# A channel attention with two MoE layers on one core: weight conversion rearranged in a hand-planned program

## Chip, core and metric

The program runs on one core of a Trainium2 chip. The metric is the device time of one execution in microseconds (us).

## What is computed

q, k and v are 6016 tokens by 256 channels, single precision. The weights come in double precision.

```
qn = q / (norm(q over tokens) + 1e-6);  kn likewise
s  = kn.T @ qn / tau                    # 256 x 256
a  = exp(s - max); a /= sum + 1e-9      # softmax over the last axis
x  = v @ a
h  = x @ w_in                           # 256 -> 2048
g  = (a0 + a1 h + a2 h^2 + a3 h^3) / (1 + |b0||h| + |b1| h^2 + 1e-6)
y  = g @ w_out                          # 2048 -> 256
out = (sigmoid(y @ w_gate) * (y @ w_val)) @ w_out2   # 256 -> 1536 -> 256
```

## The kernel before, in words

**Plan.** The kernel calls pl.op(engine, cost, vt, fn, reads, writes) for each step. Plan.schedule then runs a list schedule over these costs: among the steps that are ready on an engine, the one with the lowest vt goes first; a step with port=True also waits, in the plan, for the one port that DVE and POOL are taken to share. What comes out is a fixed order for each engine, and each engine serves its own in that order. The vt come from tables: VT (steps of the later blocks), VT0 (block 0) and WT (weights). The order on the chip is fixed by this; the times in the plan are not times of the chip.

**First part: q and k.** The 47 tiles of 128 tokens come in 15 chunks (LOADS) by DMA from SP's queue, laid out as k's first half, q, k's second half (512 columns). Each chunk lands in a buffer that a weight will fill later (STREAM). PE multiplies k by q into s_ps (s_mm, L405). ACT squares each pair of tiles (L415), DVE or POOL adds the squares to one of two sums in SBUF (L424, UNIT says which), and PE sums over the partitions with a product by ones into nrm (sum_mm, L388). Then comes a chain: square root (ACT, L464), a Newton step and reciprocals (norms, DVE), a product that spreads the norms (L477), scores (L488), exp (L498), transposes (L505), and the copy of the transposed weights of attention to SBUF (L515). The softmax's denominator goes into v's scale.

**Weights.** There are 17 pieces of 1 MB: four of W_in, four of W_out (wo), three each of wg, wv and wo2. Each holds 1024 double-precision words per partition. to_f32 turns a piece into single precision: ACT takes the high word's magnitude, scaled (Abs, L538); the low word's top bits are taken on ACT or by a shift on DVE (TOP, L541 or L545); the sign goes in on ACT, by a write into a 16-bit half of the low word (L550), or on DVE by a second step (SIGN, L556); DVE joins the parts by shift and or (L552). The result stands in a temporary in SBUF (IN_TMP, TMP). For the pieces of W_out and the second layer, split_weight makes a hi part rounded by ACT (L622) and a lo part, the difference, on DVE or POOL (LOW, L626). A W_in piece is first multiplied by the attention matrix (w_mm, L592), and its product is split from PSUM (L598 on ACT, L600 on DVE).

**Blocks.** Block 0 has 384 tokens, the eleven others 512. moe1 makes, for each of eight units j of 256 hidden columns, h in PSUM (L681 to L685), then on ACT u, abs and square (L691, L693, L695), a reciprocal's seed (L706) and an arctan (L711), on DVE six steps (v L697, w L700, Q L703, t L709, y L713, g L716), then hi (ACT, L719), lo (POOL, or DVE in block 0, L724) and the products with W_out (L732 to L742). evac_y takes y out (yhi L753, ylo L755). moe2 runs the second layer of a block while moe1 is at the next.

The DMA order of q/k chunks (x), weights (i, o, g, v, 2), constants (c) and the first v (n) is the string ORDER.

Of the kernel before, what the change touches and what calls it, by code (L numbers as in the profile page):

```python
# [225 lines left out]
def c_pool(n):  # L226
    return 0.147 + 0.002105 * n
# [7 lines left out]
def tile_channel_attention_two_moes(  # L235
# [15 lines left out]
    P = 128  # L251
# [114 lines left out]

    chunks = groups(T, LOADS[-1], LOADS[:-1])
# [4 lines left out]
    acc = {e: pl.buf("w", [P, 2, 2 * C], at=t_s) for e in "dp"}  # L372
# [23 lines left out]
    kqs = []
    for c, (t0, n) in enumerate(chunks):
        kq = pl.buf(STREAM[c], [P, n, 2 * C], at=-9000.0)
# [10 lines left out]
        pl.op(PE, 2 * n * c_pe(C, 4), t_s + c, s_mm, [kq], [s_ps])  # L409
    late = []  # L410
    for k, (c, i, n) in enumerate(units):
        kq, e = kqs[c], UNIT[k]
        fresh = k not in last and e not in of
        sq = acc[e] if fresh else pl.buf("a" if k % 2 else "s", [P, 2, 2 * C], at=t_s + k)
        pl.op(ACT, c_act(n * 2 * C, 0), t_s + c + .5, lambda kq=kq, i=i, n=n, sq=sq: nc.scalar.activation(  # L415
            out=sq.ap()[:, :n], in_=kq.ap()[:, i:i + n], func=ACTF.Square), [kq], [sq])
        if k in last:
            late.append((sq, n))
            continue
        of[e] = True  # L420
        if not fresh:
            eng = nc.vector if e == "d" else nc.gpsimd
            pl.op(DVE if e == "d" else POOL, c_dve(n * 2 * C) if e == "d" else c_pool(n * 2 * C), t_s + c + .6,
                  lambda sq=sq, n=n, x=acc[e], eng=eng: eng.tensor_tensor(  # L424
                      out=x.ap()[:, :n], in0=x.ap()[:, :n], in1=sq.ap()[:, :n], op=ALU.add),
                  [sq, acc[e]], [acc[e]], port=True)
    for e in sorted(of):
        pl.op(PE, 8 * .2, t_s + 99, sum_mm(acc[e], 2, False), [acc[e], "ones"], [nrm])
    for k, (sq, n) in enumerate(late):
        pl.op(PE, n * 4 * .2, t_n, sum_mm(sq, n, k == len(late) - 1), [sq, "ones"], [nrm])  # L430
# [16 lines left out]
    def newton(x, s, y, z, m):  # L447
# [28 lines left out]
    pl.op(DVE, 1.8, t_n, norms, [nrm, "sm_n", "cf", "ident", "sm_a"], [rn, "sm_k"], port=True)  # L476
# [52 lines left out]
    def to_f32(vt, wt, c, rkey, dst, key, n, how):  # L529
# [4 lines left out]
        def d(t=I32):  # L534
# [3 lines left out]
        pl.op(ACT, c_act(n, 0), vt, lambda: nc.scalar.activation(  # L538
            out=d(F32), in_=word(1, F32), func=ACTF.Abs, scale=DBL_EXP), [rkey], [key])
# [24 lines left out]
    ways = iter(zip(TOP, SIGN))  # L564
    win_v = words(w_in)
    for i, (c, n) in enumerate(WIN.cuts):
        load_w(WIN, win_v[:, :, c:c + n, :], i, "i")
        sb = pl.buf(IN_TMP[i], [P, 2 * CH], at=-4000.0 + i)
# [4 lines left out]
        to_f32(WT["ci"] + WT["ci_d"] * i, WIN, i, WIN.bufs[i][0], sbv, sb, 2 * n, next(ways))  # L573
# [30 lines left out]
    AT = {"o": -180.0, "g": -170.0, "v": -160.0, "2": -150.0}  # L604
    low, tmp = iter(LOW), iter(TMP)

    def split_weight(wt, src):
        x = {"wo": "o", "wg": "g", "wv": "v", "wo2": "2"}[wt.name]
        for i, (c, n) in enumerate(wt.cuts):
# [4 lines left out]
            sb = pl.buf(next(tmp), [P, 2 * CH], at=AT[x] + i)  # L614
# [248 lines left out]
```

## Time and profile before

| | us |
|---|---|
| median of 3 runs | 1256.24 (1251.53 to 1258.21) |
| the profiled execution, its own time | 1253.48 |
| its span in the profile | 1251.7 |
| first product with W_in starts (L592) | 69.10 |
| block 0's y is evacuated (L753) | 179.58 |

The profile shows one execution. Its span ends 1.8 us short of its time. Busy shares are means over the span, so they say little of a stage; windows and timelines do. A row of a timeline gives start, length, engine, line, operation, and in brackets how long the engine was idle before it and what it waited for.

### The profile page before, as it was taken

How to read it: one execution, taken by the hardware profiler on the slowest of the kernel's cores; microseconds unless marked ns; L12 is line 12 of the kernel's file. 1: busy time of each engine (PE TensorE's matmuls, PEld its weight loads, DVE VectorE, ACT ScalarE, POOL GpSimd, SP SyncE). 2: the span in 40 equal slices, each digit the busy share in tenths (PEclk: the TensorE clock that was granted, in tenths of full speed). 3: DMA queues.
4: the chain of work that ended last, by engine and by line, in shares of the span. 5: the costliest groups of instructions: out<-in, count | busy, mean ns of one | idle time of the engine just before them, and what ended most of it. 6: DMA issues, size and time to landing. Idle time of an engine off the chain costs nothing.

```text
span 1251.7 us, 13336 instructions
## 1 busy us (share of the span) xinstructions
PE 1180.9 (94%) x5170; PEld 974.4 (78%) x5170; DVE 997.4 (80%) x850; ACT 873.7 (70%) x1006; POOL 501.9 (40%) x254
## 2 busy tenths in 40 slices
PE   8762589999999999999999999999999999999998
PEld 7632578888878888888888888888888888888876
DVE  5877988848879979979979878978979979979811
ACT  6699877757757767767767757757757767767722
POOL 2301314434435435435435435435435435434422
PEclk9886699999999999999999999999999999999999
DMA  9950000000010010010010010010010000000000
GB/s 368 400 209 0 17 18 1 1 30 1 1 34 1 1 34 1 1 34 1 1 34 1 1 34 1 1 34 1 1 35 1 1 34 1 6 13 1 17 1 18
DMA packets 15601, 43.34 MB, mean 35 GB/s; under 512 B 1328, under 2 KB 1840, under 8 KB 14256
## 3 DMA queue, kind: packets, MB, share of 16 engines
q1 hardware_dynamic: 15536, 42.47, 9.0%
q8 instruction: 41, 0.67, 0.2%
q14 instruction: 24, 0.20, 0.1%
HBM read 36.31 MB, written 6.16 MB: 34 GB/s over the span
## 4 chain that ended last, share of the span: by engine, by line
PE 81%; DVE 9%; ACT 8%; DMA 1%; issue 1%; SPq 0%; DVEq 0%; ACTq 0%
PE pO L797 9%; PE pH L681 6%; PE pH L685 6%; PE pH L683 6%; PE pY L732 6%; PE pY L734 6%; PE pY L742 6%; PE pG L776 5%; PE pG L778 5%; PE pG L780 5%; PE pV L776 5%; PE pV L780 5%; PE pV L778 5%; PE pO L802 5%; DVE w L424 1%; DMA win<-in_moe_w_in_dram 1%
## 5 line engine op out<-in xcount | busy, mean ns | idle before, releaser
L790 POOL TENSOR_TENSOR lo<-sig,hi 128x512 fp32r<-128x512 f32 (+1 forms) x144 | 248.7, 1731 | 318.7 <-ACT hi L788 313.3
L724 POOL TENSOR_TENSOR lo<-w,hi 128x1024 fp32r<-128x1024 f32 (+1 forms) x90 | 219.9, 2443 | 309.3 <-ACT hi L719 240.4
L713 DVE SCALAR_TENSOR_TENSOR a<-a,s 128x1024 f32<-128x1024 f32 (+1 forms) x96 | 161.1, 1681 | 73.0 <-ACT a L711 73.0
L681 PE MATMUL pH<-vhi,win 128*128 128x512 f32 (+1 forms) x368 | 145.7, 396 | 28.5 <-DVE w L700 28.0
L732 PE MATMUL pY<-hi,wo 128*128 128x512 f32 (+1 forms) x384 | 152.3, 397 | 17.7 <-ACT hi L719 17.7
L711 ACT ACTIVATE a<-a 128x1024 f32<-128x1024 f32 (+1 forms) x96 | 99.8, 1042 | 94.2 <-DVE a L709 94.1
L709 DVE TENSOR_TENSOR a<-a,s 128x1024 f32<-128x1024 f32 (+1 forms) x96 | 162.8, 1699 | 1.8 <-ACT s L706 1.8
L693 ACT ACTIVATE a<-pH,cf 128x1024 f32<-128x1024 f32 (+1 forms) x92 | 101.8, 1107 | 83.8 <-PE pH L685 82.7
L797 PE MATMUL pO<-hi,wo 128*128 128x512 f32 (+1 forms) x576 | 151.4, 384 | 0.0
L734 PE MATMUL pY<-hi,wo 128*128 128x512 f32 (+1 forms) x384 | 151.3, 394 | 0.0
L683 PE MATMUL pH<-vlo,win 128*128 128x512 f32 (+1 forms) x368 | 144.6, 393 | 0.9 <-DVE vlo L657 0.9
L703 DVE SCALAR_TENSOR_TENSOR a<-a,s 128x1024 f32<-128x1024 f32 (+1 forms) x96 | 118.5, 1235 | 33.7 <-ACT s L695 33.4
L785 DVE TENSOR_TENSOR sig<-sig,pV 128x512 f32<-128x512 f32 (+1 forms) x144 | 96.4, 670 | 61.0 <-PE pV L780 61.0
L685 PE MATMUL pH<-vhi,win 128*128 128x512 f32 (+1 forms) x368 | 144.5, 393 | 0.0
L719 ACT ACTIVATE hi<-w 128x1024 fp32r<-128x1024 f32 (+1 forms) x96 | 100.6, 1048 | 51.8 <-PE pY L734 29.2
L716 DVE SCALAR_TENSOR_TENSOR w<-w,cf,a 128x1024 f32<-128x1024 f32 (+1 forms) x96 | 131.2, 1369 | 2.7
L797 PEld LDWEIGHTS pO<-hi,wo 128*128 128x128 f32 x576 | 107.6, 188 | 20.8
L700 DVE SCALAR_TENSOR_TENSOR w<-w,cf,pH 128x1024 f32<-128x1024 f32 (+1 forms) x92 | 116.3, 1264 | 1.2
L788 ACT ACTIVATE hi<-sig 128x512 fp32r<-128x512 f32 (+1 forms) x144 | 89.4, 628 | 37.0 <-DVE sig L785 20.4
L776 PE MATMUL pG<-yhi,wg 128*128 128x512 f32 (+1 forms) x288 | 112.2, 390 | 1.1 <-ACT yhi L753 1.1
L778 PE MATMUL pG<-ylo,wg 128*128 128x512 f32 (+1 forms) x288 | 111.4, 387 | 0.8 <-DVE ylo L755 0.8
L780 PE MATMUL pG<-yhi,wg 128*128 128x512 f32 (+1 forms) x288 | 111.4, 387 | 0.0
(176 smaller groups left out, 2334.0 us busy)
## 6 DMA issues: line engine op xcount, KB each, us to landing
wo<-in_moe_w_out_dram SPq DMA_DIRECT2D x7, 1024.0 KB, 14.4
v<-in_v_dram SPq DMA_DIRECT2D x11, 512.0 KB, 3.7
out_dram<-v SPq DMA_DIRECT2D x11, 512.0 KB, 2.8
wo<-in_kqk_dram SPq DMA_DIRECT2D x4, 1024.0 KB, 12.4
win<-in_moe_w_in_dram SPq DMA_DIRECT2D x4, 1024.0 KB, 16.7
wg<-in_kqk_dram SPq DMA_DIRECT2D x3, 1024.0 KB, 12.6
wv<-in_kqk_dram SPq DMA_DIRECT2D x3, 1024.0 KB, 17.4
wv<-in_moe_w_val_dram SPq DMA_DIRECT2D x3, 1024.0 KB, 13.8
```

The lines of the kernel that those rows point to most:

```text
L681: mm(out=hp.ap()[:, i, :n], lhsT=WIN.at(f * P, 0, z), rhs=vhi.ap()[:, z, :n], start=(z == 0), stop=False)
L683: mm(out=hp.ap()[:, i, :n], lhsT=WIN.at(f * P, 0, z), rhs=vlo.ap()[:, z, :n], start=False, stop=False)
L685: mm(out=hp.ap()[:, i, :n], lhsT=WIN.at(f * P, 1, z), rhs=vhi.ap()[:, z, :n], start=False, stop=(z == 1))
L709: pl.op(DVE, c_dve(N), vt + vp['t'] * d, lambda: nc.vector.tensor_tensor(out=V(a_), in0=V(a_), in1=V(s_), op=ALU.mult), [a_, s_], [a_], po ...
L724: lambda: e_lo.tensor_tensor(out=V(lo), in0=V(w_), in1=V(hi).bitcast(F32), op=ALU.subtract),
L732: mm(out=y_ps.ap()[:, z, :n], lhsT=WO.at(f * C, 0)[:, sl], rhs=hi.ap()[:, i, :n], start=(f == 0), stop=False)
L734: mm(out=y_ps.ap()[:, z, :n], lhsT=WO.at(f * C, 1)[:, sl], rhs=hi.ap()[:, i, :n], start=False, stop=False)
L776: mm(out=gp[i].ap()[:, :n], lhsT=wt.at(f * P, 0, z), rhs=yhi.ap()[:, z, :n], start=(z == 0), stop=False)
L778: mm(out=gp[i].ap()[:, :n], lhsT=wt.at(f * P, 0, z), rhs=ylo.ap()[:, z, :n], start=False, stop=False)
L780: mm(out=gp[i].ap()[:, :n], lhsT=wt.at(f * P, 1, z), rhs=yhi.ap()[:, z, :n], start=False, stop=(z == 1))
L790: pl.op(POOL, c_pool(n), vt + VT['lo2'] * d, lambda sg=sg, hi=hi, lo=lo: nc.gpsimd.tensor_tensor(out=lo.ap()[:, :n], in0=sg.ap()[:, :n], i ...
L797: mm(out=o_ps.ap()[:, z, :n], lhsT=WO2.at(f * C, i)[:, z * P:(z + 1) * P], rhs=hi.ap()[:, :n], start=(f == 0 and i == 0), stop=False)
```

## The change

It does five things.

1. The sign step of 7 of the 17 pieces (before 4) is a DVE step, put into the low word ahead of the join; ACT keeps 10.
2. The magnitudes of 11 pieces go into PSUM banks that are idle then (T_PS: H, Y, or 2 for the two halves in pG and pV); DVE joins from there. Squares that DVE adds up go through pH and pY too.
3. For 5 of the 15 chunks (KG is g; 13 of 47 tiles) only q is squared, and k's norms come from the diagonals of products of k with itself: s_mm multiplies 384 columns instead of 256 there, and diag_k picks the diagonals.
4. ORDER loads nine weight pieces among q and k; before, four W_in pieces stood there. The first v now comes last. The buffer of a chunk is picked by a rule instead of STREAM.
5. The hi part of 9 of 13 pieces is made by DVE (HI). The tables VT, VT0, WT are new, and block 1 and the second layer of block 0 have one of their own (VT1); the plan's cost of ACT's sign step is raised.

```diff
-ORDER = 'xxxxxxiccxxxxicxxixixxnoooovxgvgg222v'
+ORDER = 'xxvxxxvxxxxcxcgoixogxxxgixc22inovo2i'
+KG = 'ggsgssssssgsgss'
-IN_PS = 'Y2Y2'
+IN_PS = '2OYO'
-LO0 = 'dpdddddp'
+LO0 = 'ppppdpdp'
-TOP = 'adaadddaddadddddda'
-SIGN = 'ddddaaaaaaaaaaaaaa'
-LOW = 'pdddddppppddp'
+TOP = 'dadadadaaddaaddda'
+SIGN = 'daadaaadaadadaadd'
+HI = 'ddaaddddddada'
+LOW = 'pppppddpddddp'
+T_PS = 'H.2Y.Y.2HY.YH.Y.2'
...
-                    mm(out=s_ps.ap()[:, h, 0:C], lhsT=kq.ap()[:, i, h * (P + C):h * (P + C) + P],
-                       rhs=kq.ap()[:, i, P:P + C], start=(c == 0 and i == 0),
+                    lo_, hi_ = (h * P, h * P + P + C) if kg[c] else (P, P + C)
+                    mm(out=s_ps.ap()[:, h, lo_ - h * P:hi_ - h * P], lhsT=kq.ap()[:, i, h * (P + C):h * (P + C) + P],
+                       rhs=kq.ap()[:, i, lo_:hi_], start=(c == 0 and i == 0),
...
+        elif e == "d" and not direct:
+            sq = pl.buf("pH" if k % 2 else "pY", [P, 2, 512], at=t_s + c + i / 8)
...
+    def diag_k():
+        for h in range(2):
+            nc.vector.scalar_tensor_tensor(
+                out=rn.ap()[:, 2, :P], in0=s_ps.ap()[:, h, h * C:h * C + P], scalar=1.0, in1=ident, op0=ALU.mult,
+                op1=ALU.mult, accum_out=sm[:, 22 + h:23 + h])
...
+            pl.op(ACT, c_act(n // len(ts), 0), vt, lambda tv=tv, sl=sl: nc.scalar.activation(
+                out=tv(), in_=word(1, F32)[:, sl], func=ACTF.Abs, scale=DBL_EXP), [rkey], tt[1])
...
-            pl.op(ACT, c_act(n, 0), vt, lambda: nc.scalar.activation(
+            pl.op(ACT, .05 + .00215 * n, vt, lambda: nc.scalar.activation(
                 out=wt.half(c), in_=word(1, F32), func=ACTF.Copy, scale=SIGN_ONLY), [rkey, (rkey, 0)], [(rkey, 0)])
...
+                out=word(0), in0=word(1), scalar=-0x80000000, in1=word(0), op0=ALU.bitwise_and,
+                op1=ALU.bitwise_or), [rkey, (rkey, 0)], [(rkey, 0)], port=True)
+        for tv, tk, sl in ts:
+            pl.op(DVE, c_dve(n // len(ts)), vt, lambda tv=tv, sl=sl: V.scalar_tensor_tensor(
+                out=d()[:, sl], in0=tv(I32), scalar=3, in1=word(0)[:, sl], op0=ALU.logical_shift_left,
+                op1=ALU.bitwise_or), [rkey, (rkey, 0)] + tk, [key], port=t_ps == ".")
...
+            if next(high) == "a":
+                pl.op(ACT, c_act(a * m, 0), vt, lambda i=i, sv=sv: nc.scalar.activation(
+                    out=wt.part(i, 0), in_=sv(), func=ACTF.Copy), [sb], [key])
+            else:
+                pl.op(DVE, .07 + .00053 * a * m, vt, lambda i=i, sv=sv: nc.vector.tensor_copy(wt.part(i, 0), sv()),
+                      [sb], [key], port=True)
```

Three places show what the new tables do to the order. The first is SP's queue around the last chunks of q and k (rows with in_kqk_dram; a number is the buffer's). Before:

```order
L354 DMA wo_287<-in_kqk_dram 128x2048
L354 DMA win_311<-in_moe_w_in_dram 128x2x1024
L354 DMA wo_319<-in_kqk_dram 128x512
L354 DMA win_331<-in_moe_w_in_dram 128x2x1024
L354 DMA wg_339<-in_kqk_dram 128x512
L354 DMA wg_344<-in_kqk_dram 128x512
L354 DMA v<-in_v_dram 128x2x384
```

Now:

```order
L361 DMA win_335<-in_kqk_dram 128x2048
L361 DMA wo_340<-in_kqk_dram 128x512
L361 DMA wo_344<-in_kqk_dram 128x512
L361 DMA wg_346<-in_moe_w_gate_dram 128x2x1024
L361 DMA wg_366<-in_moe_w_gate_dram 128x2x1024
L361 DMA win_382<-in_moe_w_in_dram 128x2x1024
L361 DMA wv_399<-in_kqk_dram 128x512
```

Three more weight pieces stand between the last two chunks of q and k. The second place is ACT in block 0, where the first two units' seeds and arctans stand (L706 and L711; now L786 and L791). Before:

```order
L622 ACTIVATE wg_579<-yhi 128x1024
L550 ACTIVATE wo_513<-wo_513 128x1024
L550 ACTIVATE wo_547<-wo_547 128x1024
L706 ACTIVATE s<-a 128x2x384 x2
L550 ACTIVATE wo_564<-wo_564 128x1024
L538 ACTIVATE yhi<-wv_431 128x1024
L711 ACT_TABLE_LOAD
L711 ACTIVATE a<-a 128x2x384 x2
L550 ACTIVATE wv_462<-wv_462 128x1024
```

Now:

```order
L699 ACTIVATE wo_631<-hi 128x1024
L674 ACTIVATE win_636<-pO 128x512 x2
L612 ACTIVATE pV<-wo_524 128x512
L786 ACTIVATE s<-a 128x2x384
L674 ACTIVATE win_646<-pY 128x512 x2
L699 ACTIVATE wo_657<-lo 128x1024
L791 ACT_TABLE_LOAD
L791 ACTIVATE a<-a 128x2x384
L773 ACTIVATE a<-pO,cf 128x2x384
```

The last weight step on ACT is L699 of wo_657; behind it only steps of the blocks follow. The third place is DVE in the same stretch. Before:

```order
L545 TENSOR_SCALAR wv_577<-wv_577 128x1024
L552 SCALAR_TENSOR_TENSOR yhi<-yhi,wv_431 128x1024
L713 SCALAR_TENSOR_TENSOR a<-a,s 128x2x384 x2
L700 SCALAR_TENSOR_TENSOR w<-w,cf,pH 128x2x384
L700 SCALAR_TENSOR_TENSOR w<-w,cf,pO 128x2x384
L716 SCALAR_TENSOR_TENSOR w<-w,cf,a 128x2x384 x2
L552 SCALAR_TENSOR_TENSOR ylo<-ylo,wg_481 128x1024
```

Now:

```order
L676 TENSOR_TENSOR win_646<-pY,win_646 128x512 x2
L780 SCALAR_TENSOR_TENSOR w<-w,cf,pH 128x2x384
L793 SCALAR_TENSOR_TENSOR a<-a,s 128x2x384
L783 SCALAR_TENSOR_TENSOR a<-a,s 128x2x384
L796 SCALAR_TENSOR_TENSOR w<-w,cf,a 128x2x384
L777 TENSOR_TENSOR w<-w,pO 128x2x384
L789 TENSOR_TENSOR a<-a,s 128x2x384
```

Joins of weights (L552) stood between the units' steps; now the last weight step of DVE, L676 of win_646, is ahead of the first unit's w.

## Rows read from the trace of the kernel before

**Rows 1.** The page, part 1: busy time, share of the span and instructions of each engine.

```profile
PE 1180.9 (94%) x5170; PEld 974.4 (78%) x5170; DVE 997.4 (80%) x850; ACT 873.7 (70%) x1006; POOL 501.9 (40%) x254
```

**Rows 2.** Windows: stretch, its us, busy us (count) by engine, PEclk, DMA share, GB/s.

```profile
0.00:50.00 50.00, 43.42 (x198) 37.79 (x199) 35.99 (x31) 34.79 (x36) 19.58 (x14) 1.00 0.96 380
60.00:140.00 80.00, 39.99 (x135) 29.03 (x135) 61.14 (x69) 79.13 (x80) 13.61 (x5) 0.73 0.25 95
69.10:179.60 110.50, 65.70 (x237) 52.76 (x238) 92.34 (x96) 99.28 (x102) 17.74 (x7) 0.76 0.13 45
200.00:257.00 57.00, 56.60 (x282) 50.39 (x281) 44.24 (x41) 40.50 (x49) 27.13 (x16) 1.00 0.00 1
443.00:536.00 93.00, 93.00 (x410) 76.41 (x409) 79.36 (x64) 65.30 (x77) 40.84 (x20) 1.00 0.04 12
```

**Rows 3.** Timeline of PE, 0:180: start us, us, line, out<-in, count, [idle before <-releaser].

```profile
55.63 1.03 PE L388 MATMUL pV<-ones,s 128*128 128x1 f32 x8
...
69.10 5.92 PE L592 MATMUL pY<-hi,s 128*128 128x512 f32 x8 [2.13 <-ACT s L515]
...
109.01 0.66 PE L681 MATMUL pH<-vhi,win 128*128 128x384 f32 x1 [19.52 <-DVE w L700]
...
172.97 0.69 PE L732 MATMUL pY<-hi,wo 128*128 128x384 f32 x1 [2.86 <-ACT hi L719]
```

**Rows 4.** Timeline of ACT, 0:180.

```profile
47.65 0.63 ACT L415 ACTIVATE s<-wg 128x512 f32<-128x512 f32 x1 [1.85 <-DVE w L424]
...
56.70 0.17 ACT L464 ACTIVATE cf<-pV 128x4 f32<-128x4 f32 x1 [6.32 <-PE pV L388]
...
94.48 4.81 ACT L550 ACTIVATE wo<-wo 128x1024 f16<-128x1024 f32 x2
...
179.58 0.81 ACT L753 ACTIVATE yhi<-pY 128x768 fp32r<-128x768 f32 x1 [1.74 <-PE pY L742]
```

**Rows 5.** Groups by line and shape, 0:180: PE, ACT, DVE, POOL.

```profile
L405 PE MATMUL pO<-wo 128*128 128x256 f32 x84 | 20.6, 410 | 4.5 <-DMA wo<-in_kqk_dram 4.5
...
L550 ACT ACTIVATE wo<-wo 128x1024 f16<-128x1024 f32 x7 | 17.3, 2515 | 0.0
...
L538 ACT ACTIVATE v<-wo 128x1024 f32<-128x1024 f32 x5 | 5.7, 1178 | 0.9 <-DVE wo L626 0.9
L622 ACT ACTIVATE wo<-v 128x1024 fp32r<-128x1024 f32 x5 | 5.4, 1071 | 0.5 <-DVE v L552 0.3
...
L552 DVE SCALAR_TENSOR_TENSOR v<-v,wo 128x1024 int32<-128x1024 int32 x5 | 6.0, 1214 | 0.0
...
L545 DVE TENSOR_SCALAR wo<-wo 128x1024 int32<-128x1024 int32 x6 | 4.1, 688 | 0.0
...
L600 DVE TENSOR_TENSOR win<-pY,win 128x512 fp32r<-128x512 f32 x4 | 2.7, 686 | 1.9 <-ACT win L598 1.9
...
L626 POOL TENSOR_TENSOR wo<-v,wo 128x1024 fp32r<-128x1024 f32 x2 | 5.7, 2840 | 29.1 <-ACT wo L622 29.1
```

**Rows 6.** Timelines of DVE and of POOL, 0:180.

```profile
33.81 2.85 DVE L545 TENSOR_SCALAR win<-win 128x1024 int32<-128x1024 int32 x1
...
124.42 0.95 DVE L697 TENSOR_TENSOR w<-w,pH 128x768 f32<-128x768 f32 x1 [0.87 <-ACT w L691]
...
131.50 1.22 DVE L552 SCALAR_TENSOR_TENSOR ylo<-ylo,wv 128x1024 int32<-128x1024 int32 x1
...
134.50 1.22 DVE L552 SCALAR_TENSOR_TENSOR v<-v,wg 128x1024 int32<-128x1024 int32 x1
136.11 2.62 DVE L703 SCALAR_TENSOR_TENSOR a<-a,s 128x768 f32<-128x768 f32 x1 [0.40 <-ACT s L695]
...
32.89 3.22 POOL L424 TENSOR_TENSOR w<-w,a 128x1024 f32<-128x1024 f32 x1 [4.07 <-ACT a L415]
...
127.55 2.16 POOL L724 TENSOR_TENSOR lo<-w,hi 128x768 fp32r<-128x768 f32 x1 [1.60 <-ACT hi L719]
134.58 3.34 POOL L626 TENSOR_TENSOR wv<-ylo,wv 128x1024 fp32r<-128x1024 f32 x1 [4.87 <-ACT wv L622]
```

More of the change, by code (lines that the diff above doesn't have):

```diff
@@ L410, in tile_channel_attention_two_moes, with f @@
-    late = []
+        pl.op(PE, 2 * n * c_pe(P + C if kg[c] else C, 4), t_s + c, s_mm, [kq], [s_ps])
+    acc, late = {}, []
     for k, (c, i, n) in enumerate(units):
[L412 to L416, printed above, removed]
+        kq, e, g = kqs[c], UNIT[k % len(UNIT)], kg[c]
+        fresh = k not in last and (e, g) not in acc and n == (4 if g else 2)
+        direct = k in last or not fresh and (e, g) not in acc
+        if fresh:
+            sq = acc[e, g] = pl.buf("w" if e == "d" else "vhi" if g else "vlo", [P, 2, 2 * C], at=t_s + g)
+        elif e == "d" and not direct:
+            sq = pl.buf("pH" if k % 2 else "pY", [P, 2, 512], at=t_s + c + i / 8)
+        else:
+            sq = pl.buf("a" if k % 2 else "s", [P, 2, 2 * C], at=t_s + c + i / 8)
+        m = C if g else 2 * C
+        def f(t_, n=n, m=m):
+            return t_.ap().rearrange("p a c -> p (a c)")[:, :n * m].rearrange("p (a c) -> p a c", c=m)
+        pl.op(ACT, c_act(n * m, 0), t_s + c + .5, lambda kq=kq, i=i, n=n, sq=sq, f=f, g=g: nc.scalar.activation(
+            out=f(sq), in_=kq.ap()[:, i:i + n, P:P + C] if g else kq.ap()[:, i:i + n], func=ACTF.Square), [kq], [sq])
@@ L417, in tile_channel_attention_two_moes @@
         if k in last:
[L418 to L421, printed above, removed]
+            late.append((sq, n, g))
+        elif direct:
+            pl.op(PE, n * (2 if g else 4) * .2, t_s + c + .7, sum_mm(sq, n, g, False), [sq, "ones"], [nrm])
+        elif not fresh:
             eng = nc.vector if e == "d" else nc.gpsimd
[L423 to L430, printed above, removed]
+            pl.op(DVE if e == "d" else POOL, c_dve(n * m) if e == "d" else c_pool(n * m), t_s + c + .6,
+                  lambda sq=sq, x=acc[e, g], eng=eng, f=f: eng.tensor_tensor(out=f(x), in0=f(x), in1=f(sq), op=ALU.add),
+                  [sq, acc[e, g]], [acc[e, g]], port=e == "p")
@@ L432, in bcast @@
+    for (e, g), x in sorted(acc.items()):
+        pl.op(PE, 8 * .2, t_s + 99, sum_mm(x, 4 if g else 2, g, False), [x, "ones"], [nrm])
+    for k, (sq, n, g) in enumerate(late):
+        pl.op(PE, n * (2 if g else 4) * .2, t_n, sum_mm(sq, n, g, k == len(late) - 1), [sq, "ones"], [nrm])
     def bcast(src, n):
@@ L474, in norms @@
                                 scalar2=None, op0=ALU.mult)
-    pl.op(DVE, 1.8, t_n, norms, [nrm, "sm_n", "cf", "ident", "sm_a"], [rn, "sm_k"], port=True)
+    pl.op(DVE, 1.8, t_n, norms, ["sm_k2", "sm_n", "cf", "ident", "sm_a"], [rn, "sm_k"], port=True)
     pl.op(PE, c_pe(C, 4), t_n, lambda: mm(out=bc.ap()[:, 0:C], lhsT=ones, rhs=rn.ap()[:, 0, :],
@@ L602, in tile_channel_attention_two_moes @@
                 op=ALU.subtract), [ps[h], (key, 0, h)], [(key, 1, h)])
-    AT = {"o": -180.0, "g": -170.0, "v": -160.0, "2": -150.0}
-    low, tmp = iter(LOW), iter(TMP)
+    high, low, tmp = iter(HI), iter(LOW), iter(TMP)
     def split_weight(wt, src):
```

123 lines of the change are left out of this document (79 added, 44 removed).

## The prediction

> **What bounds the kernel now.** I read the page's busy shares first, then windows by stage, then the timelines of the stage that stands out, then the groups by line and shape for prices.
>
> PE is busy 94% of the span [rows 1], so little can be gained where it is already full. The windows say where it is not. From 200 us on PE is never free for long: 56.60 of 57, and in a whole block of 512 tokens 93.00 of 93 [rows 2]. In 60:140 it is busy 39.99 of 80, at a granted clock of 0.73, while ACT is busy 79.13 of those 80 [rows 2]. So the stage that can be shortened lies before 200 us: ACT sets its pace, and PE waits (19.52 us at 109.01, for a DVE step that in turn stood behind ACT) [rows 3]. What ACT does there is weight conversion standing among block 0's own steps, as with the pair of sign casts of 4.81 us at 94.48 [rows 4].
>
> Two marks cut the stage. **M1**, the first product of the attention matrix with W_in, is at 69.10 [rows 3]. **M2**, the evacuation of block 0's y, is at 179.58 [rows 4]. What PE has to do behind M2 is the same before and after: in the order 3841 rows of PE stand from the first matmul that reads yhi to the end, in both. So the time changes by as much as M2 moves, unless the later blocks' new order makes PE wait. I forecast M2, then weigh that condition as a rival.
>
> **M1, the stage that gets longer.** The last piece of q and k now comes behind nine weight pieces instead of four. A tile of q and k is 128x512 words of 4 bytes, 0.262 MB, and there are 47; a weight piece is 1.049 MB. Before: 12.3 + 4.2 = 16.5 MB, at the 380 GB/s of the first 50 us [rows 2] by 43.4 us; its square ran at 47.65, 4.2 later, of which 1.85 was idle time that DVE ended [rows 4]. After: 12.3 + 9.4 = 21.7 MB, by 57.3 us, so its square runs between 57.3 and 61.5; I take 59. With 0.63 for the square [rows 4] and two groups of sums at 1.03 [rows 3] the norms' sums end near 61.7, against 56.66 before (55.63 + 1.03). From there to M1 took 12.4 us, and the new chain differs by little: two sign casts and three Abs steps lie in it where three sign casts, an Abs step and a hi step did (2 x 2.52 + 3 x 1.18 = 8.6 against 3 x 2.52 + 1.18 + 1.07 = 9.8 [rows 5]), two small DVE steps on the diagonals come on top, and one more sign cast (2.52) stands ahead of the square root, which the sums may or may not outlast. **M1 = 74**, between 72 (no lag behind the transfer) and 79 (the full lag, and the sign cast ahead in full).
>
> Two costs lie beside this and are taken at nothing. The diagonals of k widen 26 products (13 tiles, two halves) from 256 to 384 columns: 26 x 0.205 = 5.3 us of PE, half of the 0.410 of a product [rows 5]. PE was busy 43.42 of the first 50 [rows 2]; it ends by about 53 with this, and the transfers cover it until 57; without that cover it would cost up to 5. The conversions that move ahead of M1 need ACT: 48 us of work in the 54 between the first and the last piece (18 whole squares at 1.05, nine Abs and five top-word steps at 1.18, four sign casts at 2.52, rest small). That fits, but not by much: the third rival.
>
> **M1 to M2, the stage that gets shorter.** It took 110.5 us, with ACT busy in 99.28 and DVE in 92.34 [rows 2]. In the new order no conversion stands among block 0's steps any more but for the first unit's, so I count what is left for each engine by the order.
>
> ACT: three sign casts (7.5), two whole and six half Abs (5.9), three top-word steps (3.4), four hi steps (4.3), eight W_in halves (5.0), four v casts (2.6), a table load (1.3), and eight units of block 0 of six steps, 43: 73 us. Of the 26 us that vanish, the sign casts are the largest part (ten of seventeen pieces against thirteen, and most of them now ahead of M1), then nine hi steps that went to DVE.
>
> DVE: twelve conversion steps of 1024 at 1.20 (14.4), fourteen half ones at 0.62 (8.7), four shifts and casts at 0.62 (2.5), four vlo steps (2.5), the first four steps of block 1 at 1.2 (4.8), and block 0. For that I take a run without gaps: from 124.42 to 134.50 stand ten steps of 768 columns and one conversion step, which takes 1.14 (131.50 to the next step) [rows 6], so a step takes (10.08 - 1.14)/10 = 0.894. Eight units of six and two lo steps: 50 x 0.894 = 44.7. Sum 77.6 us: **DVE is now the bound** of the stage, 4.6 ahead of ACT.
>
> On top come waits against POOL. While POOL runs, DVE steps with two operands in SBUF stretch: 2.62 instead of 0.96 at 136.11, beside the POOL step of 134.58 [rows 6]. Seven POOL steps lie in the old stage, and I count 5.6 us of stretch on DVE, 0.8 each; nine in the new one give 7. Steps that read PSUM were not stretched: the gapless run above holds a POOL step, 2.16 at 127.55 [rows 6]. More of them do now: I take 5, and 2 for other gaps. Ends: 0 and 0 (all of it falls beside PSUM steps), and 7 + 6 (a gap of 0.75 per unit). A cast of 1024 on DVE (two in this stage) is in no row: between the shift's 0.69 and a two-operand step's 1.21 [rows 5]; I take the shift, also one operand and all SBUF; the other end costs 1.
>
> The Trainium skill, "SBUF — State Buffer", section "Who interferes with whom", says that copy, cast and tensor_scalar steps in their two-port modes are shut out for the whole length of a GpSimd step. By it the nine casts moved to DVE are the change's weak spot; the sum by it is the second rival's.
>
> **M2 = 74 + 77.6 + 5 + 2 = 158.6**, which is 21.0 earlier. The profiled execution took 1253.48 (span 1251.7); minus 21.0 that is 1232.5. The median of the runs is 1256.24, 2.8 above the profiled one; on it the forecast is **1235 us**. With the low ends M2 = 149.6, 1226; with the high ends 79 + 78.6 + 13 = 170.6, 1247.
>
> **Rivals.**
> 1. *More.* The PSUM operands take away all stretch, ACT keeps up: M2 near 150, 1226. For it: the steps that read PSUM. Against it: t, y, Q and g of block 0 keep both operands in SBUF.
> 2. *DVE shut out.* Each one-operand step meets a POOL step, as the shift at 33.81 did: 2.85 instead of 0.69, beside POOL's 32.89 [rows 6]. Four such steps behind M1 lose 8.6, and the two-operand ones the full 7.2: 15.8 instead of 5, M2 169.4, 1246. Against it: nine POOL steps of some 2.84 [rows 5] fill under a third of the 85 us.
> 3. *No gain.* The conversions ahead of M1 don't fit: each queue is served in order, so an ACT step that waits for a late transfer holds the squares behind it, and POOL's sums, at 2.4 to 3.2 each, hold DVE. M1 at 90 gives M2 174.6, 1251, within what counts as no change.
> 4. *Slower.* The new tables reorder every block, not only the first. PE is full there, but DVE is busy 79.36 and POOL 40.84 of 93 [rows 2], and a unit's hi, lo and products hang in a chain; where PE meets a hi that isn't there it stands 2.86 us, as at 172.97 [rows 3]. Once more in each of eleven blocks: 31.5, and 1235 + 31.5 = 1267. It decides from 27 us on, 2.5 per block. Against it: DVE keeps 13.6 us of slack in a block, and the new order has the same steps per block, in much the same sequence.
>
> **How the numbers follow.** A measurement of this kernel can tell about 0.5% from no change, 6.3 us (1250.0 to 1262.5). Forecast 0.66 (1228 to 1243), rival one 0.10, two 0.10, three 0.07, four 0.07. The first three cases lie below 1250: faster 0.86; rival three is same, 0.07; rival four slower, 0.07. The range 1225 to 1249 takes in the forecast, rivals one and two and the ends of the unknown costs, and leaves out three and four and a little of the tails.
>
> **What would show it.** In the new profile: M1 between 72 and 79; no sign cast and no DMA-fed conversion behind the second unit of block 0; DVE busy for over 95% of M1 to M2 while ACT has gaps; M2 near 159; blocks from the third on still 93 us apart with PE full. An M2 over 170 with long one-operand DVE steps beside POOL would show rival two; an M1 over 85, rival three; PE idle inside later blocks, rival four. The forecast is wrong if M2 moves by 21 and the time doesn't.

## The result: 18 us faster, and the profile after

The changed kernel takes 1238.01 us (median of 4 runs, 1235.97 to 1242.28), the kernel before 1256.65 beside it: a ratio of 0.9863, with a 95% interval of 0.9824 to 0.9902. Run again beside later experiments it took 1236.69 (4 runs) against 1253.45, 0.9867 (0.9845 to 0.9889). The forecast was 1235, in a range of 1225 to 1249: faster, by about what was said. But M2 moved less than forecast, and the reason why is the more useful part.

The profiled execution of the changed kernel is the slowest of its first four (1242.28, span 1240.5), so the two profiles stand 11.2 apart and the medians 18.6. A second profile of the same kernel, taken with the runs below, has a span of 1235.7.

Page, part 1, and windows of the changed kernel (first profile), which answer to [rows 1, 2]:

```profile
PE 1192.8 (96%) x5202; PEld 978.7 (79%) x5202; DVE 999.0 (81%) x855; ACT 861.9 (69%) x998; POOL 523.0 (42%) x262
```

```profile
0.00:50.00 50.00, 45.67 (x182) 34.85 (x183) 25.67 (x18) 37.99 (x33) 26.48 (x17) 1.00 0.97 385
60.00:140.00 80.00, 54.86 (x193) 40.77 (x193) 70.03 (x105) 68.28 (x80) 16.58 (x8) 0.78 0.28 107
80.60:165.70 85.10, 62.58 (x237) 47.64 (x238) 78.06 (x88) 69.40 (x83) 19.68 (x9) 0.89 0.05 14
443.00:536.00 93.00, 93.00 (x410) 76.54 (x409) 78.86 (x63) 65.85 (x77) 41.12 (x20) 1.00 0.04 12
240.00:257.00 17.00, 13.71 (x47) 9.53 (x46) 12.11 (x11) 10.09 (x11) 2.40 (x1) 0.87 0.17 53
```

In 60:140 PE is busy for 54.86 us where it was for 39.99, and ACT is no longer full there (68.28 instead of 79.13). From M1 to M2 DVE is now the busiest engine, 78.06 of 85.10, where ACT was, 99.28 of 110.50. A later block is as full as before, 93.00 of 93.

Timeline of PE, changed kernel, answering to [rows 3]:

```profile
52.16 2.32 PE L426 MATMUL pO<-wo 128*128 128x384 f32 x8
55.60 1.95 PE L400 MATMUL pV<-ones,w 128*128 128x1 f32 x16 [1.11 <-DVE w L456]
57.41 3.12 PE L400 MATMUL pV<-ones,vlo 128*128 128x1 f32 x16
60.39 3.55 PE L400 MATMUL pV<-ones,vhi 128*128 128x1 f32 x16
63.80 2.05 PE L426 MATMUL pO<-wv 128*128 128x256 f32 x4
65.65 1.71 PE L400 MATMUL pV<-ones,a 128*128 128x1 f32 x8
67.21 1.84 PE L400 MATMUL pV<-ones,s 128*128 128x1 f32 x8
...
80.61 3.78 PE L668 MATMUL pG<-lo,s 128*128 128x512 f32 x4 [1.91 <-ACT s L560]
```

Timeline of ACT, changed kernel, answering to [rows 4]:

```profile
58.69 0.61 ACT L447 ACTIVATE s<-wv 128x512 f32<-128x512 f32 x1
...
69.35 0.20 ACT L509 ACTIVATE cf<-sm 128x4 f32<-128x4 f32 x1 [3.20 <-DVE sm L506]
...
165.71 0.81 ACT L833 ACTIVATE yhi<-pY 128x768 fp32r<-128x768 f32 x1 [1.62 <-PE pY L822]
```

M1 is at 80.61 (before 69.10), M2 at 165.71 (before 179.58). So 11.5 us are lost ahead of M1, 25.4 won from M1 to M2, and M2 is 13.9 earlier. The table gives the same marks for every kernel that was run; "rest" is the span minus M2. In the kernels whose order is the changed kernel's the rest is 1070 to 1075, so M2 of one profile orders them more finely than medians of few runs do. The spans of the profiles follow M2: with more early work on ACT (e3) M2 is 11.1 later than in the changed kernel's second profile, and the span 11.3 longer.

| kernel | M1 | M1 to M2 | M2 | rest | median us (runs) | ratio to before (95%) |
|---|---|---|---|---|---|---|
| before | 69.10 | 110.48 | 179.58 | 1072.1 | 1256.65 (4) | |
| changed | 80.61 | 85.10 | 165.71 | 1074.8 | 1238.01 (4) | 0.9863 (0.9824 to 0.9902) |
| changed, again | 81.48 | 84.33 | 165.81 | 1069.9 | 1236.69 (4) | 0.9867 (0.9845 to 0.9889) |
| e1 fewer sums | 76.69 | 84.32 | 161.01 | 1070.1 | 1235.44 (4) | 0.9857 (0.9835 to 0.9878) |
| e2 ACT + 3 casts late | 81.39 | 89.74 | 171.13 | 1071.5 | 1243.31 (6) | 0.9922 (0.9899 to 0.9946) |
| e3 ACT + 4 casts early | 89.89 | 86.98 | 176.87 | 1070.1 | 1248.11 (10) | 0.9954 (0.9938 to 0.9971) |
| e4 DVE + 6 steps late | 80.72 | 94.52 | 175.24 | 1070.1 | 1249.92 (12) | 0.9960 (0.9942 to 0.9978) |
| e5 hi on ACT, same order | 79.35 | 84.13 | 163.48 | 1070.2 | 1235.67 (4) | 0.9871 (0.9836 to 0.9906) |
| folded sums | 78.09 | 84.99 | 163.08 | 1071.5 | 1235.52 (4) | 0.9848 (0.9827 to 0.9870) |
| before, honest sign cost | 68.52 | 102.78 | 171.30 | 1081.5 | 1251.23 (10) | 0.9984 (0.9968 to 0.9999) |
| signs undone, new plan | 78.73 | 100.30 | 179.03 | 1079.9 | 1260.85 (4) | 1.0061 (1.0043 to 1.0079) |
| PSUM undone, new plan | 79.37 | 109.89 | 189.26 | 1078.5 | 1270.56 (4) | 1.0140 (1.0123 to 1.0157) |
| diagonals undone, new plan | 94.42 | 78.13 | 172.55 | 1071.8 | 1245.67 (4) | 0.9937 (0.9921 to 0.9954) |
| hi undone, new plan | 81.36 | 100.62 | 181.98 | 1078.9 | 1263.49 (4) | 1.0075 (1.0057 to 1.0093) |

### The profile page after: what moved, and what is told of

Same layout as the page of the kernel before. It is cut to its first block, busy times and chain, and to the rows that moved or that the text cites. A ratio compares the mean times of both kernels' runs of the same rounds, so it can differ in the third digit from the quotient of the medians.

```text
span 1240.5 us, 13259 instructions
## 1 busy us (share of the span) xinstructions
PE 1192.8 (96%) x5202; PEld 978.7 (79%) x5202; DVE 999.0 (81%) x855; ACT 861.9 (69%) x998; POOL 523.0 (42%) x262
## 4 chain that ended last, share of the span: by engine, by line
PE 87%; ACT 5%; DMA 3%; DVE 2%; issue 1%; POOL 1%; SPq 0%; POOLq 0%; ACTq 0%; DVEq 0%
PE pO L878 10%; PE pH L761 7%; PE pH L763 7%; PE pH L765 7%; PE pY L822 6%; PE pY L812 6%; PE pY L814 6%; PE pG L857 5%; PE pG L859 5%; PE pG L861 5%; PE pV L857 5%; PE pV L859 5%; PE pV L861 5%; PE pO L883 5%; DMA wg<-in_moe_w_gate_dram 1%
## 5 line engine op out<-in xcount | busy, mean ns | idle before, releaser
L804 POOL TENSOR_TENSOR lo<-w,hi 128x1024 fp32r<-128x1024 f32 (+1 forms) x94 | 230.7, 2454 | 280.7 <-ACT hi L799 222.5
L793 DVE SCALAR_TENSOR_TENSOR a<-a,s 128x1024 f32<-128x1024 f32 (+1 forms) x96 | 170.8, 1779 | 51.8 <-ACT a L791 51.6
L812 PE MATMUL pY<-hi,wo 128*128 128x512 f32 (+1 forms) x384 | 149.0, 388 | 12.9 <-ACT hi L799 12.9
L783 DVE SCALAR_TENSOR_TENSOR a<-a,s 128x1024 f32<-128x1024 f32 (+1 forms) x96 | 115.5, 1203 | 47.9 <-ACT s L775 45.5
L796 DVE SCALAR_TENSOR_TENSOR w<-w,cf,a 128x1024 f32<-128x1024 f32 (+1 forms) x96 | 151.1, 1574 | 2.8
L814 PE MATMUL pY<-hi,wo 128*128 128x512 f32 (+1 forms) x384 | 148.3, 386 | 0.0
L789 DVE TENSOR_TENSOR a<-a,s 128x1024 f32<-128x1024 f32 (+1 forms) x96 | 144.1, 1501 | 0.0
L791 ACT ACTIVATE a<-a 128x1024 f32<-128x1024 f32 (+1 forms) x96 | 100.0, 1042 | 61.6 <-DVE a L789 61.6
L857 PE MATMUL pG<-yhi,wg 128*128 128x512 f32 (+1 forms) x288 | 112.6, 391 | 2.7 <-ACT yhi L833 2.2
L864 ACT ACTIVATE sig<-pG 128x512 f32<-128x512 f32 (+1 forms) x144 | 85.1, 591 | 38.4 <-PE pG L861 24.0
```

Of the source, the lines that this page charges most:

```text
L793: pl.op(DVE, c_dve(N), vt + vp['y'] * d, lambda: stt(out=V(a_), in0=V(a_), scalar=ATAN_C, in1=V(s_), op0=ALU.add, op1=ALU.mult), [a_, s_], ...
L796: pl.op(DVE, c_dve(N, 1), vt + vp['g'] * d, lambda: stt(out=V(w_), in0=V(w_), scalar=col(A0), in1=V(a_), op0=ALU.add, op1=ALU.mult), [w_, ...
L804: lambda: e_lo.tensor_tensor(out=V(lo), in0=V(w_), in1=V(hi).bitcast(F32), op=ALU.subtract),
L812: mm(out=y_ps.ap()[:, z, :n], lhsT=WO.at(f * C, 0)[:, sl], rhs=hi.ap()[:, i, :n], start=(f == 0), stop=False)
L814: mm(out=y_ps.ap()[:, z, :n], lhsT=WO.at(f * C, 1)[:, sl], rhs=hi.ap()[:, i, :n], start=False, stop=False)
L857: mm(out=gp[i].ap()[:, :n], lhsT=wt.at(f * P, 0, z), rhs=yhi.ap()[:, z, :n], start=(z == 0), stop=False)
```

## Experiments in the order of the changed kernel

Theory: M1 sets M2 and M2 the time; PE's sums hold M1; DVE bounds M1 to M2 with ACT close behind. In these runs every engine keeps the changed kernel's order, but for the steps named.

**Fewer sums.**

```diff
-        pl.op(PE, 8 * .2, t_s + 99, sum_mm(x, 4 if g else 2, g, False), [x, "ones"], [nrm])
+        pl.op(PE, 8 * .2, t_s + 99, sum_mm(x, 4 if g else 2, g, False) if e == "d" else (lambda: None), [x, "ones"], [nrm])
```

> The changed kernel with the 32 one-column products of POOL's two accumulators (vlo and vhi, 6.67 us on PE from 57.41) left out, so k's and q's norms lack those tiles. Theory (M1 is late because these products stand between the last chunk and the square root, and the time goes with M2, M2 with M1): the norms' sums end about 5 to 6 us earlier than 69.05, M1 near 75 instead of 80.6, M2 near 160.5 instead of 165.7, the time 4 to 6 us below the changed kernel's, near 1233. Rival (the conversions on ACT and DVE set M2 whatever M1 does): M1 earlier, but M2 and the time by less than 2 us.

M1 came to 76.69 and M2 to 161.01, 4.7 earlier than in the changed kernel, and the profiled span is 4.6 below that of the second profile (1231.1 against 1235.7). For M1 and M2 the theory holds and the rival falls. The times don't decide between them: the median is 2.6 and 1.3 below the two medians of the changed kernel, where the theory said 4 to 6 and the rival less than 2, and the intervals of the ratios overlap. (The 32 are rows of PE; two rows make a product.) M1 gains less than the sums do, since a sign cast then stands between them and the square root. Timeline of ACT in this run:

```profile
63.11 2.46 ACT L624 ACTIVATE wg<-wg 128x1024 f16<-128x1024 f32 x1
65.47 0.21 ACT L509 ACTIVATE cf<-sm 128x4 f32<-128x4 f32 x1
```

The square root starts as the cast ends; in the changed kernel it waited 3.20 us for the sums.

**More on ACT, late and early.** The early run names other pieces (wv 0, wg 0, wo 0, wo 1) in the same line.

```diff
-            pl.op(ACT, .05 + .00215 * n, vt, lambda: nc.scalar.activation(
-                out=wt.half(c), in_=word(1, F32), func=ACTF.Copy, scale=SIGN_ONLY), [rkey, (rkey, 0)], [(rkey, 0)])
+            def sign():
+                for _ in range(2 if (wt.name, c) in (("wo", 2), ("win", 2), ("wv", 2)) else 1):
+                    nc.scalar.activation(out=wt.half(c), in_=word(1, F32), func=ACTF.Copy, scale=SIGN_ONLY)
+
+            pl.op(ACT, .05 + .00215 * n, vt, sign, [rkey, (rkey, 0)], [(rkey, 0)])
```

> The changed kernel with ACT's sign cast done twice for three pieces that are converted around and behind M1 (the third of W_out, of W_in and of wv): 3 x 2.52 = 7.5 us more on ACT, nothing else. Theory (DVE bounds M1 to M2 with ACT close behind): DVE takes up part of it, the time 1 to 4 us longer than the changed kernel's. Rival (ACT still bounds M1 to M2, as before the change): the whole 7 to 8 us, near 1245.

> The changed kernel with ACT's sign cast done twice for four pieces that are converted among q and k (the first of wv, of wg and of W_out and the second of W_out): 4 x 2.52 = 10 us more on ACT ahead of M1, nothing else. Theory (ahead of M1 the transfers, and behind them PE's sums, set the end; ACT has room): 0 to 3 us longer. Rival (the conversions fill ACT ahead of M1 as well): M1 later by 6 us or more and the time 6 to 10 us longer.

Late, 7.5 us more on ACT made M1 to M2 longer by 4.6 to 5.4 (against either profile of the changed kernel): ACT has 2 to 3 us to spare there, not more. That lies between the theory's upper end and the rival. Early, 10 us more moved M1 by 8.4 to 9.3 and the time by 10 to 11: the theory falls here, the rival holds. Ahead of M1 there is no room for added work on ACT.

**More on DVE, late.**

```diff
+            def sign():
+                for _ in range(3 if (wt.name, c) in (("wo", 3), ("wo2", 2), ("win", 3)) else 1):
+                    V.scalar_tensor_tensor(out=word(0), in0=word(1), scalar=-0x80000000, in1=word(0),
+                                           op0=ALU.bitwise_and, op1=ALU.bitwise_or)
```

> The changed kernel with DVE's sign step done three times for three pieces that are converted behind M1 (the last of W_out, of W_in and of wo2): 6 steps of about 1.14 us, 6.8 us more on DVE, nothing else. Theory (DVE bounds M1 to M2): 5 to 7 us longer than the changed kernel's, near 1244. Rival (ACT bounds it): DVE takes it into its gaps, less than 2 us longer.

Timeline of DVE in this run:

```profile
85.56 5.79 DVE L629 SCALAR_TENSOR_TENSOR wo<-wo 128x1024 int32<-128x1024 int32 x3
...
94.85 3.74 DVE L629 SCALAR_TENSOR_TENSOR wo<-wo 128x1024 int32<-128x1024 int32 x3
...
101.90 3.74 DVE L629 SCALAR_TENSOR_TENSOR win<-win 128x1024 int32<-128x1024 int32 x3
```

The three groups take 13.27 us where single steps took 3.67 (1.22 or 1.23 each), so 9.6 more, not 6.8: repeated in place, a step takes 1.25, and the first group ran partly beside POOL. M1 to M2 grew by 9.4 to 10.2 (against either profile): DVE passes on all of it, where ACT passed on about two thirds. DVE is the bound of the stage, as forecast. The median grew by 12 to 13, not by the 5 to 7 expected; in the profiles the span grew by 9.6 (1245.3 against 1235.7), and why the medians grew by more is not explained.

**Hi parts back on ACT, at the same places.**

```diff
-                pl.op(DVE, .07 + .00053 * a * m, vt, lambda i=i, sv=sv: nc.vector.tensor_copy(wt.part(i, 0), sv()),
+                pl.op(DVE, .07 + .00053 * a * m, vt, lambda i=i, sv=sv: nc.scalar.activation(
+                    out=wt.part(i, 0), in_=sv(), func=ACTF.Copy),
```

> The changed kernel with its nine casts for hi parts done by ACT (1.07 each) instead of DVE, each at the same place of the order; the order of everything else stays (the run before, with the plan made again, mixed this with a new order). In the trace seven of the nine lie ahead of M1 and two behind it. Theory (ACT's work ahead of M1 passes to M1 nearly whole, as with the doubled sign casts; behind M1 DVE bounds): seven steps, 7.5 us, of which the first two or three fall into ACT's waits for transfers: M1 4 to 7 us later, M1 to M2 within 1.5 us of 85, M2 and the time 4 to 8 us later, near 1243. Rival A (the worth is what the planned-again run showed, M2 at 182): 14 us or more. Rival B (moving hi to DVE gained nothing, because DVE is just as full): less than 2 us.

M1 came 2.1 earlier than in the changed kernel's second profile (1.3 than in the first) and M2 2.3 (2.2); the median is 1.0 lower, too little to tell by the times. The theory of M1 falls, and rival A with it; rival B holds. So the nine casts gained nothing on DVE. The timelines of DVE and POOL say why. The changed kernel, second profile:

```profile
42.08 0.69 DVE L702 CAST wg<-s 128x1024 fp32r<-128x1024 f32 x1
...
43.41 3.27 DVE L627 SCALAR_TENSOR_TENSOR win<-win 128x1024 int32<-128x1024 int32 x1
46.61 3.41 DVE L631 SCALAR_TENSOR_TENSOR hi<-hi,wo 128x1024 int32<-128x1024 int32 x1
...
52.95 1.81 DVE L702 CAST wo<-yhi 128x1024 fp32r<-128x1024 f32 x1
54.68 1.21 DVE L456 TENSOR_TENSOR w<-w,pH 128x1024 f32<-128x1024 f32 x1
...
42.91 2.70 POOL L706 TENSOR_TENSOR wg<-s,wg 128x1024 fp32r<-128x1024 f32 x1 [5.16 <-DVE wg L702]
46.08 2.86 POOL L456 TENSOR_TENSOR vhi<-vhi,a 128x1024 f32<-128x1024 f32 x1 [0.48 <-ACT a L447]
...
54.16 2.82 POOL L456 TENSOR_TENSOR vlo<-vlo,s 128x1024 f32<-128x1024 f32 x1
```

With the casts on ACT:

```profile
41.90 1.23 DVE L627 SCALAR_TENSOR_TENSOR win<-win 128x1024 int32<-128x1024 int32 x1
43.37 1.23 DVE L631 SCALAR_TENSOR_TENSOR hi<-hi,wo 128x1024 int32<-128x1024 int32 x1 [0.24 <-ACT wo L624]
...
50.77 1.23 DVE L631 SCALAR_TENSOR_TENSOR yhi<-pY,wo 128x1024 int32<-128x1024 int32 x1 [4.33 <-ACT wo L624]
53.48 1.22 DVE L456 TENSOR_TENSOR w<-w,pH 128x1024 f32<-128x1024 f32 x1 [1.47 <-ACT pH L447]
...
44.26 2.57 POOL L707 TENSOR_TENSOR wg<-s,wg 128x1024 fp32r<-128x1024 f32 x1 [6.71 <-ACT wg L702]
```

A cast on DVE releases POOL's lo step at once (2.70 at 42.91 in the changed kernel). DVE's next two steps, with both operands in SBUF, run beside POOL, the first beside this lo step and the second beside POOL's next one, an add of squares: 3.27 and 3.41 instead of 1.23. On ACT the cast ends later, POOL starts at 44.26, and by then one of the two is done and the other has begun. DVE then waits for ACT instead, and its last add into w still starts 1.2 earlier (0.9 against the first profile). PE, which waits for that add in the changed kernel, doesn't stop here. Its timeline, with the casts on ACT:

```profile
54.75 1.95 PE L400 MATMUL pV<-ones,w 128*128 128x1 f32 x16
56.56 1.93 PE L400 MATMUL pV<-ones,vlo 128*128 128x1 f32 x16
58.35 3.41 PE L400 MATMUL pV<-ones,vhi 128*128 128x1 f32 x16
```

The group of vlo takes 1.93, at full clock, where it took 3.12 and 3.55 in the two profiles of the changed kernel. So part of M1's gain is the earlier add and part the clock, which falls one group later here.

**Folded sums.** Three adds of 512 on DVE take the place of 24 of PE's rows (the expectation says 20), and the last chunk's product moves up. The core of the edit, in the loop that emits the planned steps:

```diff
+        order = pl.schedule()
+        order.remove(sums[0])
+        order.remove(last_mm)
+        order.insert(order.index(sums["p", True]), last_mm)
...
+            if o is dve:
+                half(acc["p", False])
+            if o is sums["p", True]:
+                half(acc["p", True])
             o.fn()
+            if o is last_sq:
+                half(late[1][0], late[0][0])
```

> The changed kernel with fewer one-column products in the norms and nothing left out: DVE folds the two halves of each of POOL's accumulators, and the squares of the second-last chunk into those of the last, ahead of the products (three adds of 512, some 0.65 us each); PE then has 24 such products where it had 40 behind the first accumulator, and the last chunk's product by q is put ahead of vhi's. All else stands in the order of the changed kernel. Theory (PE's sums at half clock hold M1, and M2 goes with M1): 20 rows of some 0.22 us go, the sums end 3 to 4 us earlier than 69.05, M1 near 77, M2 near 162, the time 2.5 to 4 us below the changed kernel's, some 1234. Rival (DVE, which is full at 50 to 60 us, gives it back): the sums end within 1 us of before and the time moves by less than 1.5 us.

> The changed kernel itself once more, beside the others on one chip, as what they are compared with: 1236 to 1240 us, M2 within 0.5 us of 165.7.

Timeline of PE, folded sums:

```profile
58.27 1.05 PE L400 MATMUL pV<-ones,vlo 128*128 128x1 f32 x8 [0.83 <-DVE vlo L460]
59.18 2.00 PE L426 MATMUL pO<-wv 128*128 128x256 f32 x4
62.16 1.87 PE L400 MATMUL pV<-ones,vhi 128*128 128x1 f32 x8 [0.98 <-DVE vhi L460]
63.89 1.85 PE L400 MATMUL pV<-ones,s 128*128 128x1 f32 x8
...
78.09 3.78 PE L675 MATMUL pG<-lo,s 128*128 128x512 f32 x4 [1.88 <-ACT s L567]
```

The sums end at 65.74 instead of 69.05 (69.96 in the second profile), M1 is 2.5 to 3.4 earlier, M2 2.7 earlier: for these the theory, at its lower end. By the medians of four runs each the gain is 1.2 us (1235.52 against 1236.69), less than the 2.5 to 4 of the theory, and these runs can't tell it from none. It is the lowest ratio of all, though its interval overlaps the changed kernel's. Folded sums together with e5's casts were not tried.

## Experiments with the plan made again

Here one part of the change is undone, or done alone, and the list schedule runs anew; the tables remain those made for another set of steps. So such a run shows the part and the misfit of the tables together.

**The plan's honest cost, alone**, on the kernel before:

```diff
-            pl.op(ACT, c_act(n, 0), vt, lambda: nc.scalar.activation(
+            pl.op(ACT, .05 + .00215 * n, vt, lambda: nc.scalar.activation(
                 out=wt.half(c), in_=word(1, F32), func=ACTF.Copy, scale=SIGN_ONLY), [rkey, (rkey, 0)], [(rkey, 0)])
```

> The kernel before with one thing of the change alone: the plan's cost of ACT's sign step is raised to what it takes; the plan is made again with the old tables. Theory (the gain comes from ACT work that goes away or moves ahead of M1: three sign casts and nine hi steps fewer, 17 us less on ACT): the steps stay the same, so the order can win little: M2 within 5 us of 179.6, the time within 5 us of before. Rival (the old order was bad because its plan took a sign cast for 1 us instead of 2.5): M2 earlier by 8 us or more and the time 8 to 16 us below before.

M2 came 8.3 earlier, which speaks for the rival, but the rest grew by 9.4, and the time is lower by only 0.2% (0.9984). The better order ahead of M2 was paid for behind it: the y of block 1 is evacuated at 263.51, before at 257.82. This cost alone, with the old tables, is not what made the change faster.

**Signs, PSUM banks, diagonals and hi parts undone**, each from the changed kernel:

```diff
-SIGN = 'daadaaadaadadaadd'
+SIGN = 'ddddaaaaaaaaaaaaa'
```

```diff
-T_PS = 'H.2Y.Y.2HY.YH.Y.2'
+T_PS = '.................'
```

```diff
-KG = 'ggsgssssssgsgss'
+KG = 'gssssssssssssss'
```

```diff
-HI = 'ddaaddddddada'
+HI = 'aaaaaaaaaaaaa'
```

> The changed kernel with the sign step of the pieces as before: 4 on DVE, 13 on ACT, planned again with the changed tables. Theory (ACT's share of the conversions sets the stage): three more casts of 2.52 on ACT, three steps of 1.2 less on DVE: M2 and the time 4 to 10 us later than the changed kernel's (more would be the tables' misfit). Rival (DVE bounds it, so giving DVE less helps): 0 to 4 us earlier.

> The changed kernel with all magnitudes in SBUF temporaries (no PSUM banks for them), planned again with the changed tables. Theory (the gain is engine time on ACT): no engine's steps change in number, M2 and the time 0 to 4 us later. Rival (the PSUM banks carry the gain, because they free temporaries and keep DVE's joins out of POOL's way): 8 us or more later.

> The changed kernel with k's squares taken by ACT again in all chunks but the first (diagonals for 2 of 47 tiles instead of 13), planned again with the changed tables. PE has 4.5 us less to do among q and k (11 x 2 x 0.205), ACT 22 half tiles of squares more (about 5 us with their adds on DVE or POOL). Theory (PE's late end holds M1, but ACT has little room ahead of M1 either, as the run with doubled early sign casts showed): nearly even, M1 and the time within 4 us of the changed kernel's. Rival (the diagonals only cost PE time): 4 to 6 us earlier.

> The changed kernel with all 13 hi parts made by ACT, as before, planned again with the changed tables: nine steps of 1.07 back on ACT, nine casts of 0.69 to 1.86 off DVE. Theory (DVE bounds M1 to M2 and ACT is some 3 us behind it, as the runs with added steps showed): about five of the nine lie behind M1, so ACT becomes the bound by some 2 us, and the four ahead of M1 add some 4: 4 to 8 us longer than the changed kernel's. Rival (the casts, stretched beside POOL, cost DVE more than they save ACT): 0 to 4 us shorter.

All four are slower than the changed kernel, by 9 to 34 us, and each by more than the theory expected. How much of that is misfit the hi part shows: planned again it cost 27 us, at fixed places none. (Its expectation also counted wrongly: seven of the nine casts lie ahead of M1.) So these figures are no prices of the parts, and which parts bring the 25.4 us between M1 and M2 is not shown. What two of the new orders waited for can still be read. Timeline of PE with the diagonals undone:

```profile
71.53 3.58 PE L400 MATMUL pV<-ones,w 128*128 128x1 f32 x16 [12.76 <-DVE w L456]
```

The sums wait 12.76 us for DVE's last add, which the new order put behind a row of weight steps: order ate more than the 4.5 us that PE saved. Timelines of ACT and of PE with the PSUM banks undone:

```profile
123.76 1.08 ACT L674 ACTIVATE win<-pO 128x512 fp32r<-128x512 f32 x2 [7.79 <-PE pO L668]
```

```profile
126.22 0.45 PE L761 MATMUL pO<-vhi,win 128*128 128x384 f32 x1 [2.50 <-DVE win L676]
```

Three W_in pieces share one temporary (lo) there, and the last one is split at 123.76; in the changed kernel it is done by 112. From M1 to M2 neither ACT (72.98 of 109.90) nor DVE (86.52) is full. The row of 126.22 shows a unit's product that waits for the last of these weights. That speaks for the rival, that the banks carry much of the gain because they free temporaries, but how much stays open, since this order too is a misfit.

## Why the prediction was right, and which terms were off

**M1 to M2: the bound right, the sum right in part by luck.** The sum said 84.6; measured were 85.1 and 84.3. DVE is the bound (the run with added DVE steps passed on all 9.4), ACT 2 to 3 us behind it where the sum said 4.6. But the terms miss in both directions. DVE was busy for 78.06, of which 2.3 are stretch (two steps of block 0, 1.67 and 2.61 instead of 0.95 and 1.01), where the sum had 77.6 of work and 5 of stretch; and it stood idle for 7.0, nearly all of it in waits for ACT, where the sum had 2. So it was busy 92% of the stage, not over 95%.

**M1: the term that failed.** The forecast was 74, between 72 and 79; measured were 80.61 and 81.48. "The norms' sums end near 61.7", from "two groups of sums at 1.03" behind the last square. The square itself ran at 58.69, forecast 59. But the groups of vlo, vhi and the last chunk's product stood ahead of these two, and at half clock the two took 1.71 and 1.84. They ended at 69.05: 7.4 late, of which M1 shows 6.6. At full clock, where PE went through 16 such rows in 1.81 (55.60 to 57.41) and through 16 rows of products of 256 columns in 3.62 (at 48.71), the same rows would have ended near 63.7 (an estimate): some 2 of the 7.4 are rows that the sum left out, and some 5 the half clock. The run without POOL's sums and the folded one, both with an earlier M1 and M2, show that term. It was in the code (three accumulators, before two) and in the order, and the sum didn't count it. The rows of before warned of it too: there the stretch from the end of the last square (48.28) to the end of the sums (56.66) took 8.4 us, where the sum allowed 2.1; with 8.4 it would have come to 68.0.

**Diagonals "taken at nothing": nothing seen, with little to spare.** The wide products took 52 rows at 0.106 more (0.486 against 0.380), 5.5 us. The prediction's 5.3 is near that by luck: it took half of 0.410 for each product, but 0.410 is the length of a row, and two rows make a product. PE was full from 10 us to 50, and these products ended at 54.5, not at 53. Yet the sums then waited 1.11 us for DVE's last add, so in this trace it isn't the products that held them. With the hi parts on ACT the add came earlier, and the sums began right behind the products (54.75): there is no cover beyond that. What the diagonals cost or save in all is not shown, since their only run has another order.

**"That fits, but not by much"**, of ACT ahead of M1: right. Added work there went to M1 nearly whole (8.4 to 9.3 of 10). What the prediction did not see is that DVE is just as tight between 40 and 57 us, so that work changed over from ACT to DVE there won nothing.

**M2 moves by 21: it moved by 13.9**, the 7.1 missing being M1's 6.6 and 0.5. That the time still came within 3 us of 1235 is luck: 13.9 less than 1256.24 is 1242.3, which lies in the range but not near its middle. The medians differ by 16.8 to 18.6, 3 to 5 more than M2. The rest behind M2 doesn't explain that by the order of the steps: it is 1072.1 before and 1069.9 to 1074.8 after. It varies by that much between executions of one kernel (the last section says with what), and so do the times, 1235.97 to 1242.28 for the changed kernel and 1251.53 to 1258.21 for the one before. Why the medians differ by more than M2 is not settled beyond this.

**Rivals.** *More* did not come, M2 being far from 150. *No gain* and *slower* did not come either: later blocks stand 92.9 apart as before. *DVE shut out* came true in kind, but not where it was priced. Behind M1 (first profile) no one-operand step was stretched, and of the two-operand steps only two. Ahead of M1, where it had no price, two-operand steps stretched to 3.4 and casts to 1.86. The Trainium skill, "SBUF — State Buffer", section "Who interferes with whom", also says that a DVE step with two SBUF inputs contends with a GpSimd step that reads SBUF, and one with at most one SBUF input outside the two-port modes does not. The rows above agree: 3.27 and 3.41 with both operands in SBUF, 1.21 for the add at 54.68 that takes one from PSUM, beside POOL's step of 54.16.

## What to carry to other kernels

Count every instruction that stands on the serial path between two stages, and at the clock that this stretch has, not at that of the busy one before it: here sums that the forecast left out, and the half clock at which they ran, took 7 of the 21 us that it promised. When work is moved between two engines that feed each other, ask what its earlier result will start, since a faster step can release a third engine that slows the first. And undo a part of a scheduled kernel at fixed places: with the schedule made again, one part seemed worth 27 us that was worth nothing.

## What the hardware showed that was not expected

- The granted clock was 1.00 up to 55 us, 0.89 in 50:60 and 0.50 in 60:80 (of two levels, 1.2 and 2.4 GHz), although PE was busy in 9.06 of the 10 us from 60 to 70, for the most part with one-column products. PE had been idle for 1.11 us before these began. A group of 16 such rows took 1.95 us at 55.60 and 3.55 at 60.39. In the run with the hi parts on ACT, where PE was not idle before them, the second group still ran at full clock (1.93 at 56.56).
- The rest behind M2 varies between executions of one kernel by 4.9 us (1074.8 and 1069.9), and dips of the granted clock account for nearly all of it. In the first profile the clock is 0.87 in 240:257, where PE is idle for 3.3 of 17 us (0.66 in 250:260), and again 0.87 in 1185:1195, behind 1.9 us of idle time; in the second, with the same idle times, it stays at 1.00 in both places. By PE's busy time and the clock in these stretches the two dips cost some 4.6 us (an estimate). The kernel before has two such dips behind M2 in its profile, of some 3 us. The mean clock of whole executions goes with their times: 0.983 in the fastest of the changed kernel's first four (1235.97), 0.979 in the slowest (1242.28). The second profile:

```profile
240.00:257.00 17.00, 13.71 (x55) 9.62 (x54) 12.53 (x12) 9.97 (x11) 2.40 (x2) 1.00 0.16 54
```

- ACT gains next to nothing by writing to PSUM: squares of 1024 took 1.01 to 1.03 into PSUM and 1.04 to 1.13 into SBUF, magnitudes 1.08 to 1.25 against 1.13 to 1.21.
